# Weights split by casting and accumulating transfers, and Q, K and x moved by matmuls in the first groups of a recurrence-and-experts kernel

## The chip, the cores and the metric

The kernel runs on one core of a Trainium2 chip. The metric is the device time of one execution in microseconds, over several runs; a profiled execution gives the traces. TensorE (PE in the profile) multiplies matrices and writes PSUM; its weight loads have a row of their own (PEld). DVE and ACT do the elementwise work, POOL (GpSimd) fills and selects, and transfers are issued by SP's queue and POOL's.

## The reference

A linear recurrence per head with a complex decay, then a mixture of four dense experts:

```python
mag = np.sqrt(a_re * a_re + a_im * a_im)
scale = np.minimum(mag, 0.999) / (mag + 1e-06)       # a_re, a_im times scale
for t in range(S):
    S_re, S_im = ar * S_re - ai * S_im + kv, ar * S_im + ai * S_re   # kv = outer(k[t], v[t])
    y[:, :, t] = np.einsum('bhd,bhde->bhe', q[:, :, t], S_re)
x = y as [B*S, H*D] = [3072, 384]
p = domain_probs / (domain_probs.sum(-1) + 1e-09)
for e in range(4):
    out += p[:, e:e+1] * (np.maximum(x @ w1[e], 0) @ w2[e])          # w1[e]: 384 x 1024, w2[e]: 1024 x 384
```

There are 4 batches, 8 heads of 48, 768 steps. All data are float32.

## The kernel before

**Tiles.** The 3072 rows are cut into 12 groups of 256 (three per batch), a group into two chunks of 128. In the first part of the kernel every group goes through the recurrence ("attention" in the code) and then through experts 0 and 1; in the second part (lines 559 to 631) blocks of 512 rows go through experts 2 and 3 and the output is written. The second part isn't touched, except for a name.

**Weights.** The 32 weight tiles `w[i]` are 128 x 768: 384 columns of w1, then 384 rows' worth of w2. TensorE multiplies in its 32-bit matmul type (fp32r in the profile), which is shorter than float32, so each tile is held as a high part `whi` and a remainder `wlo`, and every product is a sum of three. `split_w` (L112) makes the two: a transfer by SP brings the tile (`wst`), ACT casts it (L115), and in the first part TensorE forms source minus high part in PSUM, by the identity and its negative (L125, L128), whence ACT copies it (L129). All 16 tiles of experts 0 and 1 are split before the first MoE matmul.

**The recurrence.** For each group DVE and ACT normalize the decay (`norm`, L276), form running products of it (`prefix`, L304) and from them the scaled queries Q and keys K (`finish`, L326), with the channels (head times 48) on partitions in three blocks of 128. The attention wants heads side by side instead, 48 rows at partitions 0 (real) and 64 (imaginary). That move goes through DRAM: `q_d`, `k_d` are written (L378) and read back into `Qst`, `Kst` (L383). In `chunk`, `increment` turns K (L411), copies it to `KT` and multiplies it with v (L416); `scores` multiplies `Kst` with `Qst` (L430) and DVE applies a mask (L433); `values` adds scores times v (L446) and state times Q (L442) in PSUM and copies y out (L454). y takes another trip through DRAM (`y_d`, L486, and `load_x`, L135) to come back as x with channels on partitions; `split_x` (L138) makes its high part `xha` (ACT) and remainder `xla` (DVE).

**The experts.** `moe1` goes over eight steps of two tiles: 18 matmuls of w1 (`w1_step`, L152), ReLU on ACT (L161), remainder on DVE (L162), 12 matmuls of w2 (`w2_step`, L171). `done` scales the sum and POOL stores it (L497).

**Order.** Each engine runs its instructions in the order that a scheduler gave them when the kernel was built; the program's order is its priority. `behind` fixes single orders. `attention` is a generator: while the block of group g - 1 runs, `between` lets one piece of group g's attention be issued ahead of steps `first`, `first + 1` and `first + 2`, with `first = max(2, 5 - g)` (L539). Group 0 has no block to hide behind. The probabilities `pr` are loaded by POOL at the start (L88) and reduced on DVE (L527). Tiles with the tag `tmp` share four buffers, `K` and `qk` have one, `A` two.

Of the kernel before, what the change touches and what calls it, by code (L numbers as in the profile page):

```python
# [29 lines left out]
NST = 4  # L30
# [25 lines left out]
NPRE = 10  # L56
NMID = 12
# [3 lines left out]
def fast_path(ctx, tc, qkP, aP, vP, probsP, w, out, flag):  # L61
# [8 lines left out]
    ident = const.tile([P, P], F32, name="ident")  # L70
    make_identity(nc, ident)
    nident = const.tile([P, P], F32R, name="nident")
    nc.scalar.activation(nident, ident, AF.Copy, scale=-1.0)
# [14 lines left out]
    nc.gpsimd.dma_start(pr, probsP.rearrange("(n p) e -> p n e", p=P))  # L88
# [5 lines left out]
    wts = {}  # L94

# [16 lines left out]
    def split_w(i, src, ps=None, prev=None, prev_pe=None):  # L112
        hi = wpool.tile([P, 2 * HD], F32R, tag="whi", name=f"whi{i}")
        lo = wpool.tile([P, 2 * HD], F32R, tag="wlo", name=f"wlo{i}")
        ins = nc.scalar.activation(hi, src, AF.Copy)  # L115
        if prev is not None:
            behind(ins, prev)
        if ps is None:
            nc.vector.tensor_tensor(lo, src, hi, op=ALU.subtract)
        else:  # L120
            pool, tag = ps
            for u in range(2):
                us = slice(u * HD, (u + 1) * HD)
                lp = pool.tile([P, HD], F32, tag=tag, name=f"lp{i}_{u}")
                ins = nc.tensor.matmul(lp, ident, src[:, us], start=True, stop=False)  # L125
                if prev_pe is not None:
                    behind(ins, prev_pe)
                last_pe = nc.tensor.matmul(lp, nident, hi[:, us], start=False, stop=True)  # L128
                nc.scalar.activation(lo[:, us], lp, AF.Copy)  # L129
        wts[i] = (hi, lo)  # L130
        return last_pe if ps is not None else None

    def load_x(g):
        x = moe.tile([P, NJ, G], F32, tag="x", name=f"xa{g}", bufs=1)
        nc.sync.dma_start(x, y_d[g].rearrange("(j p) t -> p j t", p=P))  # L135
        return x

    def split_x(g, x):  # L138
        xh = moe.tile([P, NJ, G], F32R, tag="xh", name=f"xha{g}")
        xl = moe.tile([P, NJ, G], F32R, tag="xl", name=f"xla{g}")  # L140
        tc.keep_in_program_order(nc.scalar.activation(xh, x, AF.Copy))  # L141
        tc.keep_in_program_order(nc.vector.tensor_tensor(xl, x, xh, op=ALU.subtract))
# [59 lines left out]
    with ExitStack() as c1:  # L202
# [4 lines left out]
        mask = big.tile([P, C], F32, name="mask")  # L207
# [6 lines left out]
        for i in range(SEG):  # L214
            nc.gpsimd.dma_start(maskp[i * CS:(i + 1) * CS], mask_d[:, i, :])
# [9 lines left out]
        nc.gpsimd.memset(Qst[32:IM], 0.0)  # L225
        nc.gpsimd.memset(Kst[32:IM], 0.0)
        nc.gpsimd.memset(KT, 0.0)
        nc.gpsimd.memset(P2, 0.0)
        nc.gpsimd.memset(TA, 0.0)

# [22 lines left out]
        def tmp(name):  # L253
            return big.tile([P, 2, NJ * G], F32, tag="tmp", name=name, bufs=TMP)

        def cmul(x, br, bi, shape, nm):
# [6 lines left out]
            v1 = tmp(f"{nm}a")[:, :, :n].rearrange(pat, **kw)  # L263
            v2 = tmp(f"{nm}b")[:, :, :n].rearrange(pat, **kw)
# [11 lines left out]
        def norm(g, A, parts=((0, SEG),), prev=(None, None)):  # L276
            s = tmp(f"s{g}")
            u = tmp(f"u{g}")
            for n, (lo, hi) in enumerate(parts):
# [5 lines left out]
                nc.scalar.activation(L, Af[:, 1], AF.Square)  # L285
# [5 lines left out]
                if n > 0:  # L291
                    behind(ins[0], idn)
                nc.scalar.activation(L, m2, AF.Ln, bias=m2b)
                nc.scalar.activation(y0, L, AF.Exp, scale=-0.5)
# [9 lines left out]
        def prefix(g, A, cuts=(1, NS)):  # L304
            for i in range(1, SEG):
# [6 lines left out]
                nc.vector.tensor_tensor(x[:, 1], z[:, 1, 0], z[:, 0, 1], op=ALU.add)  # L312
            k = 1
            while k < NS:
                nb = MS // (2 * k)
                Al = A[:, :, SEG - 1, :].rearrange("p c (b s) -> p c b s", s=2 * k)
                br, bi = (Al[:, c, :, k - 1:k].broadcast_to([P, nb, k]) for c in range(2))
                cmul(Al[:, :, :, k:], br, bi, [nb, k], f"sk{g}_{k}")
                k *= 2
            As = A.rearrange("p c i (j s) -> p c i j s", j=NJ)  # L320
# [5 lines left out]
        def finish(g, A, qk, parts=((0, CG),)):  # L326
            Q = big.tile([P, 2, NR, C + 1], F32, tag="tmp", name=f"Q{g}", bufs=TMP)
            K = big.tile([P, 2, NR, C], F32, tag="K", name=f"K{g}", bufs=1)
            s = tmp(f"s2{g}")
            u = tmp(f"u2{g}")  # L330
# [19 lines left out]
            for lo, hi in parts:  # L350
# [11 lines left out]
                if hi == CG:  # L362
                    nc.scalar.activation(Q[:, :, :, C].rearrange("p c (j n) -> p c j n", n=CG)[:, :, :, lo:],
                                         A[:, :, SEG - 1, NS - 1::NS].unsqueeze(3).broadcast_to([P, 2, NJ, hi - lo]),
                                         AF.Copy)
                a2, i0, t, kn = (some(x, lo, hi) for x in (a2a, i0a, ta, qk[:, 1]))
# [6 lines left out]
                scr = []  # L373
                for x, nm, w in ((Q, "q", C + 1 if hi == CG else C), (K, "k", C)):
                    dt = dram.tile([2, HD, hi - lo, w], F32, name=f"{nm}_d{g}_{lo}")
                    for c in range(2):
                        xs = x[:, c].rearrange("p (j n) t -> p j n t", n=CG)[:, :, lo:hi, :w]
# [18 lines left out]
        def chunk(g, c, K, y):  # L396
# [8 lines left out]
            def increment():  # L405
                if last:
                    return
# [416 lines left out]
```

## Time and profile before

| | us |
|---|---|
| median of 3 runs (lowest, highest) | 1032.83 (1031.87, 1033.28) |
| profiled execution, its own time | 1035.97 |
| its span, first to last instruction | 1034.2 |
| TensorE busy in it | 988.0 (96%) |
| DVE, ACT busy | 596.5, 358.9 |
| first MoE matmul starts | 74.27 |

A page has the busy time by engine, the span in 40 slices with digits for tenths, the transfers, the chain of work that ended last, and groups of instructions. `x` counts instructions; a time in brackets behind an arrow is idle time in front of an instruction and what ended it. In a group's line the first number behind the bar is busy time in us, the second the mean of one in ns. A float32 matmul shows as two records. Stretches are given in us from the start of the span.

### The profile page before, as it was taken

What the parts mean: (1) busy time and instruction counts of PE and PEld (TensorE: products, weight loads), DVE (VectorE), ACT (ScalarE), POOL (GpSimd) and SP (SyncE); (2) the same over time, 40 slices, a digit from 0 to 9 for tenths busy, and PEclk for the clock granted to TensorE, in tenths of its full rate; (3) what the DMA queues carried; (4) which work ended last, traced back from release to release, by engine and by line L of the source; (5) the groups of instructions that cost most, each with busy time, mean ns of one, the idle gap of its engine ahead of it and who ended that gap; (6) DMA issues with size and microseconds to landing.
All of it is one profiled execution on the core that took longest, in us unless ns stands there. A gap on an engine that the chain in (4) does not pass through costs nothing.

```text
span 1034.2 us, 15984 instructions
## 1 busy us (share of the span) xinstructions
PE 988.0 (96%) x6522; PEld 920.8 (89%) x6522; DVE 596.5 (58%) x1201; ACT 358.9 (35%) x647; POOL 27.8 (3%) x51
## 2 busy tenths in 40 slices
PE   4599889999999999999999999999999999999997
PEld 2379889898999999999999999999999999999996
DVE  6788877798988998888982264232232232321221
ACT  6845335352634635355342254121111111111110
POOL 4100000000000000000000000000000000000000
PEclk9989999999999999999999999999999999999999
DMA  7837372745658455483653493012030010100000
GB/s 257 217 113 155 107 197 80 191 115 141 165 139 199 120 149 152 120 203 126 145 123 78 129 360 123 1 41 82 1 110 13 22 71 1 61 1 1 31 1 34
DMA packets 79378, 113.12 MB, mean 109 GB/s; under 512 B 5440, under 2 KB 64496, under 8 KB 79296
## 3 DMA queue, kind: packets, MB, share of 16 engines
q1 hardware_dynamic: 76768, 101.61, 35.5%
q0 software_dynamic: 2528, 10.41, 2.8%
q8 instruction: 53, 0.87, 0.4%
q14 instruction: 29, 0.24, 0.1%
HBM read 74.11 MB, written 37.88 MB: 108 GB/s over the span
## 4 chain that ended last, share of the span: by engine, by line
PE 88%; DMA 6%; DVE 3%; ACT 1%; issue 1%; SPq 0%; DVEq 0%; POOL 0%; ACTq 0%; POOLq 0%
PE pob L598 19%; PE phb L585 19%; PE ph L152 18%; PE po L171 17%; PE sc L430 5%; PE dp L416 2%; PE yp L446 2%; PE yp L442 2%; DMA Kst<-k_d 2%; DMA k_d<-K 1%; PE ktp L411 1%; PE lp L125 1%; DMA pr<-probsP 1%; DMA q_d<-Q 1%; DMA xa<-y_d 1%
## 5 line engine op out<-in xcount | busy, mean ns | idle before, releaser
L591 DVE SCALAR_TENSOR_TENSOR hlb<-phb,hhb 128x512 fp32r<-128x512 f32 x96 | 66.3, 691 | 247.2 <-ACT hhb L590 247.2
L590 ACT ACTIVATE hhb<-phb 128x512 fp32r<-128x512 f32 x96 | 57.4, 598 | 314.2 <-PE phb L585 299.9
L171 PE MATMUL po<-whi,hh 128*128 128x384 f32 x384 | 129.2, 339 | 1.1 <-ACT hh L161 1.1
L598 PE MATMUL pob<-wlo,hhb 128*128 128x384 f32 x384 | 129.3, 337 | 0.0
L171 PE MATMUL po<-wlo,hh 128*128 128x384 f32 x384 | 129.1, 336 | 0.0
L598 PE MATMUL pob<-whi,hhb 128*128 128x384 f32 x384 | 128.9, 336 | 0.0
L171 PE MATMUL po<-whi,hl 128*128 128x384 f32 x384 | 123.1, 338 | 0.5 <-DVE hl L162 0.5
L598 PE MATMUL pob<-whi,hlb 128*128 128x384 f32 x384 | 117.8, 336 | 0.0
L152 PE MATMUL ph<-xha,whi 128*128 128x256 f32 x576 | 105.6, 288 | 4.1 <-ACT xha L141 4.1
L161 ACT ACTIVATE hh<-ph 128x512 fp32r<-128x512 f32 x96 | 57.2, 596 | 149.7 <-PE ph L152 146.1
L152 PE MATMUL ph<-xla,whi 128*128 128x256 f32 x576 | 103.5, 286 | 0.0
L152 PE MATMUL ph<-xha,wlo 128*128 128x256 f32 x576 | 101.4, 284 | 0.0
L162 DVE SCALAR_TENSOR_TENSOR hl<-ph,hh 128x512 fp32r<-128x512 f32 x96 | 66.0, 688 | 51.0 <-ACT hh L161 50.3
L152 PEld LDWEIGHTS ph<-xha,whi 128*128 128x128 f32 x576 | 87.2, 191 | 6.2 <-ACT xha L141 4.9
L585 PE MATMUL phb<-xhb,whi 128*128 128x512 f32 x288 | 91.8, 392 | 0.0
L152 PEld LDWEIGHTS ph<-xla,whi 128*128 128x128 f32 x576 | 83.6, 192 | 0.7 <-issue 0.6
L152 PEld LDWEIGHTS ph<-xha,wlo 128*128 128x128 f32 x576 | 83.2, 191 | 0.2 <-issue 0.2
L585 PE MATMUL phb<-xlb,whi 128*128 128x512 f32 x288 | 83.4, 392 | 0.0
L585 PE MATMUL phb<-xhb,wlo 128*128 128x512 f32 x288 | 82.1, 393 | 0.0
L598 PEld LDWEIGHTS pob<-wlo,hhb 128*128 128x128 f32 x384 | 72.1, 188 | 3.5
L598 PEld LDWEIGHTS pob<-whi,hhb 128*128 128x128 f32 x384 | 72.1, 188 | 3.4
L171 PEld LDWEIGHTS po<-whi,hh 128*128 128x128 f32 x384 | 72.6, 189 | 1.6 <-ACT hh L161 1.4
(142 smaller groups left out, 1568.9 us busy)
## 6 DMA issues: line engine op xcount, KB each, us to landing
wst<-w SPq DMA_DIRECT2D x32, 384.0 KB, 4.8
qk<-qkP SPq DMA_DIRECT2D x24, 384.0 KB, 7.0
acc_d<-acc POOLq DMA_DIRECT2D x24, 384.0 KB, 4.5
prev<-acc_d SPq DMA_DIRECT2D x24, 384.0 KB, 4.8
q_d<-Q SPq DMA_DIRECT2D x22, 387.0 KB, 3.8
Qst<-q_d SPq DMA_DIRECT2D x22, 387.0 KB, 5.6
A<-aP SPq DMA_DIRECT2D x22, 384.0 KB, 8.7
k_d<-K SPq DMA_DIRECT2D x22, 384.0 KB, 3.0
```

Source lines behind the costliest of these rows:

```text
L152: ins = nc.tensor.matmul(ph[:, u, :], wt[:, j * P:(j + 1) * P], xt[:, j, :], start=(n == 0), stop=(n == 3 * NJ - 1))
L161: nc.scalar.activation(hh, ph, AF.Relu)
L162: nc.vector.scalar_tensor_tensor(hl, ph, 0.0, hh, op0=ALU.max, op1=ALU.subtract)
L171: nc.tensor.matmul(po[t], ht[:, u, t * P:(t + 1) * P], wt[:, HD:], start=(i % FE == 0 and n == 0), stop=(i % FE == FE - 1 and n == 2))
L416: ins = nc.tensor.matmul(d_ps[:, h, :], KT[:, h, :], vc[:, h * D:(h + 1) * D], start=True, stop=True)
L430: nc.tensor.matmul(s_ps[:, h, :], Kc[:, hf * 4 + h, :], Qc[:, hf * 4 + h, :], start=True, stop=True)
L442: ins = nc.tensor.matmul(yo, state[g, c][:, h, :], Qc[:, h, :], start=True, stop=False)
L446: ins = nc.tensor.matmul(yo, vc[:, h * D:(h + 1) * D], sc[h // 4][:, h % 4, :], start=first, stop=True)
L585: nc.tensor.matmul(ph, wt[:, j * P:(j + 1) * P], xt[:, j, :], start=(n == 0), stop=(n == 3 * NJ - 1))
L590: nc.scalar.activation(hh, ph, AF.Relu)
L591: nc.vector.scalar_tensor_tensor(hl, ph, 0.0, hh, op0=ALU.max, op1=ALU.subtract)
L598: nc.tensor.matmul(po[t], ht[:, t * P:(t + 1) * P], wt[:, HD:], start=(i % FE == 0 and n == 0), stop=(i % FE == FE - 1 and n == 2))
```

## The change

**Weights of experts 0 and 1.** POOL issues 16 transfers that cast from float32 to the matmul type (`cast`) and so write `whi` directly. ACT writes its negative into `wlo`, and a second transfer by POOL adds the tile onto it. SP's loads, the identity matmuls and the copies from PSUM go. A small copy on POOL (`tick`) waits for the last part of the first decay tile ahead of the casts. The first ten negated copies are placed behind the first normalization, the other six behind xh of group 0. At the end the check that chooses between this path and a general one (a loop over the 768 steps) also asks that the largest remainder of tile 0 is above zero on every partition.

```diff
-    def split_w(i, src, ps=None, prev=None, prev_pe=None):
...
+    def cast(i):
+        whi[i] = wpool.tile([P, 2 * HD], F32R, tag="whi", name=f"whi{i}")
+        nc.gpsimd.dma_start(whi[i], w[i])
...
+    def split_w(i, prev=None):
+        lo = wpool.tile([P, 2 * HD], F32R, tag="wlo", name=f"wlo{i}")
+        ins = nc.scalar.activation(lo, whi[i].bitcast(F32), AF.Copy, scale=-1.0)
+        if prev is not None:
+            behind(ins, prev)
+        nc.gpsimd.dma_start(lo, w[i], accum_op=ALU.add)
+        wts[i] = (whi[i], lo)
```

**Q and K of groups 0 and 1 (`NSEL = 2`).** Q of chunk 0 of group 0, and K of chunk 1 of both groups, are moved by `pick`: matmuls whose stationary operand is 48 columns of a wide identity. K of chunk 0 is turned for the increment as before, and turned back head by head from `KT` into `Kst` (`turned_back`). The other parts of Q keep the trip through DRAM, all of it by SP. `blank` writes zeros into the rows between the two halves, since one copy now takes all 112 rows.

```diff
+        def blank(ps):
+            n, w = ps.shape[1:]
+            nc.tensor.matmul(ps[32:IM], zero, ident[0:1, 0:1].unsqueeze(2).broadcast_to([1, n, w]),
+                             start=True, stop=True)
+
+        def pick(g, nm, X, dst, s, w):
+            n = 4 if w == C else 3
+            for h0 in range(0, H, n):
+                hs = range(h0, min(h0 + n, H))
+                ps = ps_a.tile([M, len(hs), w], F32, tag="pa", name=f"{nm}p{g}_{s}_{h0}")
+                blank(ps)
+                for h in hs:
+                    js = [j for j in range(NJ) if -D < h * D - j * P < P]
+                    for j in js:
+                        o = 32 + h * D - j * P
+                        for c in range(2):
+                            nc.tensor.matmul(ps[c * IM:c * IM + D, h - h0, :], wide[:, o:o + D],
+                                             X[:, c, j * CG + s, :w], start=(j == js[0]), stop=(j == js[-1]))
+                nc.scalar.activation(dst[:, h0:h0 + len(hs), s, :w], ps, AF.Copy)
...
+            def turned_back():
+                for h0 in range(0, H, 4):
+                    ps = ps_a.tile([M, 4, C], F32, tag="pa", name=f"kp{g}_{c}_{h0}")
+                    for h in range(4):
+                        nc.tensor.transpose(ps[:, h, :], KT[:, h0 + h, :], ident)
+                    nc.scalar.activation(Kst[:, h0:h0 + 4, c, :], ps, AF.Copy)
```

**x of groups 0, 1 and 2 (`XSEL = 3`).** `turn_x` makes x in PSUM from y by matmuls with slices of a band of ones, six per chunk, and `split_x` reads it there. `y_d` is still written, for the second part; `values` blanks the rows between the halves of its PSUM tile for these groups (one more matmul per chunk).

```diff
+        def turn_x(g, c, y):
+            xp = ps_a.tile([P, NJ, C], F32, tag="pa", name=f"xp{g}_{c}")
+            for j in range(NJ):
+                ps = [p for p in range(HP) if -HOFF < 2 * D * p - P * j < P]
+                for p in ps:
+                    o = HOFF - (2 * D * p - P * j)
+                    state["xp"] = nc.tensor.matmul(xp[:, j, :], band[:, o:o + P], y[:, p, c * C:(c + 1) * C],
+                                                   start=(p == ps[0]), stop=(p == ps[-1]))
+            return slice(c * C, (c + 1) * C), xp
```

**Order.** For groups 0 and 1, prefix and finish run chunk by chunk (`front`), with the attention's pieces between them, and the last piece (turning K of chunk 1, its increment, the rotation of the state) comes behind the split of x. In `norm` of group 0 the squares of the second half are placed behind the first half's Exp. The steps at which pieces come are a table.

```diff
+FIRST = {1: 5, 2: 4, 3: 3, 4: 2}
...
+        def near_attention(g, QK):
+            Q, K = QK
+            y = small.tile([M, HP, G], F32, tag="y", name=f"y{g}")
+            (turn0, back0, inc0, sc0, val0), (turn1, back1, inc1, sc1, val1) = (chunk(g, c, K, y) for c in range(CG))
+            if g == 0:
+                pick(g, "q", Q, Qst, 0, C)
+                yield
+                landed = trip(f"q_d{g}", Q, Qst, 1)()
+            else:
+                landed = trip(f"q_d{g}", Q, Qst)()
+            yield landed
+            turn0()
+            back0()
+            sc0()
+            yield
+            pick(g, "k", K, Kst, 1, C)
+            inc0()
+            val0()
+            sc1()
+            xs = [turn_x(g, 0, y)]
+            val1()
+            xs.append(turn_x(g, 1, y))
+            yield xs
+            store_y(g, y)
+            t_factors()
+            turn1()
+            inc1()
+            rotate(g)
...
+        behind(nc.vector.reduce_sum(prs, pr, axis=mybir.AxisListType.X), ld)
```

`ld` is the last K product of group 0. Besides, the eight loads of the permuted mask move from POOL's queue to SP's, small products in `cmul` share one temporary tile, one wide identity takes the place of two, and POOL's fills change with the tiles (no fill of `Kst`, half of the one of `Qst`, a new band).

More of the change, by code (lines that the diff above doesn't have):

```diff
@@ L29 @@
 E1 = 2
-NST = 4
+NST = 6
 TMP = 4
@@ L403, in chunk, with turned @@
             sc = []
-            def increment():
-                if last:
+            def turned():
+                if last and g >= NSEL:
                     return
```

255 lines of the change are left out of this document (151 added, 104 removed).

## The prediction

> **What bounds the kernel now.** I read the page first, then busy time and granted clock by stretches, then the chain that ended last, then the waits of DVE and TensorE.
>
> ```profile
> span 1034.2 us, 15984 instructions
> ...
> PE   4599889999999999999999999999999999999997
> ```
>
> TensorE is the bound, but not everywhere: its row is full from the third slice on, apart from two 8s, and half empty in the first two. The stretches say it in microseconds (TensorE first, then its weight loads, DVE, ACT, POOL, granted clock, DMA share, GB/s).
>
> ```profile
> 10.00:20.00 10.00, 6.19 (x12) 3.02 (x11) 9.86 (x27) 7.97 (x16) 3.87 (x8) 1.00 0.96 367
> 52.00:74.20 22.20, 20.82 (x134) 16.25 (x132) 17.75 (x50) 10.38 (x23) 0.00 (x0) 0.87 0.42 127
> 74.20:120.00 45.80, 45.66 (x372) 44.09 (x373) 41.75 (x88) 19.59 (x37) 0.58 (x1) 1.00 0.52 126
> 120.00:166.00 46.00, 38.87 (x305) 36.37 (x303) 35.25 (x79) 18.57 (x35) 1.10 (x2) 0.96 0.51 138
> 166.00:212.00 46.00, 43.92 (x335) 42.37 (x334) 36.69 (x79) 20.71 (x39) 1.08 (x2) 0.96 0.55 147
> 212.00:258.00 46.00, 44.48 (x357) 42.92 (x355) 38.80 (x84) 20.00 (x38) 0.54 (x1) 0.96 0.54 141
> ```
>
> From 74.2 to 258 TensorE is idle for 0.14 + 7.13 + 2.08 + 1.52 = 10.9 us, and in three stretches it has 0.96 of its clock, 3 x 46 x 0.04 = 5.5 us more: 16.4 us lost. So the end is the start of the first MoE matmul, plus TensorE's work behind it, plus these losses. The chain shows how that start comes about (start, length).
>
> ```profile
> 1.39 8.25 DMA pr<-probsP
> ...
> 11.64 0.61 ACT s L293
> ...
> 12.85 0.42 ACT u L294
> ...
> 37.80 0.33 DVE u L367
> 38.13 7.53 DMA k_d<-K
> ...
> 46.67 4.67 DMA Kst<-k_d
> ...
> 72.86 0.50 ACT wlo L129
> ...
> 73.37 0.85 ACT xha L141
> ...
> 74.27 1.82 PE ph L152 x13
> ```
>
> Three things stretch it: DVE waits for the router probabilities, K takes a round trip through DRAM, and the weight splits stand in front of xh. DVE's waits before 75, and the end of its K:
>
> ```profile
> DVE scs L433 <- PE sc L430: 7.2, 2, 6.8
> DVE prs L527 <- DMA pr<-probsP: 4.8, 1, 4.8
> ```
>
> ```profile
> 39.48 1.03 DVE L371 TENSOR_TENSOR K<-A,u 128x384 f32<-128x384 f32 x2
> ```
>
> TensorE's waits after 74.2, by who ended them:
>
> ```profile
> PE sc L430 <- DMA Kst<-k_d: 4.9, 2, 2.8
> PE ph L152 <- ACT xha L141: 4.1, 2, 2.6
> PE sc L430 <- issue: 2.3, 3, 1.5
> ```
>
> **The head, step by step.** The reduction over the probabilities moves behind the last K product, so DVE no longer sits idle for 4.8 us until the transfer lands at 9.6. Late next are ACT's Ln and Exp of the first half (0.61 and 0.42), which the change puts ahead of the squares of the second half: normalizing begins near 6 in place of 9.7. I move K's end by 4 us, from 40.5 to 36.5. The first chunk's K is ready one tail earlier (2.7 us, from 37.8 to 40.5 in the trace), at 33.8.
>
> From there no transfer of K and no reload of x is on the path; TensorE is. Its prices:
>
> ```profile
> L430 PE MATMUL sc<-Qst,Kst 112*128 112x128 f32 x384 | 55.0, 299 | 15.9 <-DMA Kst<-k_d 13.5 <-issue 2.3
> L446 PE MATMUL yp<-scs,v 128*48 128x128 f32 x384 | 36.1, 275 | 0.0
> L416 PE MATMUL dp<-v,KT 128*112 128x48 f32 x320 | 34.4, 258 | 1.3 <-issue 1.3
> ...
> L125 PE MATMUL lp<-wst,ident 128*128 128x384 f32 x64 | 29.5, 550 | 13.5 <-DMA wst<-w 9.6 <-ACT wlo L129 3.7
> ...
> L411 PE MATMUL ktp<-ident,K 128*128 128x128 f32 x120 | 18.1, 276 | 0.0
> ```
>
> ```profile
> 109.05 0.39 PE L446 MATMUL yp<-scs,v 128*48 128x128 f32 x4
> 109.27 0.39 PE L442 MATMUL yp<-Qst,G 112*48 112x128 f32 x4
> ```
>
> A float32 matmul is two records. A full one on 128 columns costs at most 2 x 55.0/384 = 0.29 us; I take 0.25, since that union holds each group's drain. A 48-wide one costs between 0.11 (four records, two matmuls, start 0.22 apart) and 0.19 (2 x 36.1/384); the selection matmuls alternate between the same two halves of the output, so 0.11. A transpose is at most 18.1/120 = 0.15, taken as 0.12; an increment matmul at most 2 x 34.4/320 = 0.21, taken as 0.2. A matmul that blanks the rows between the halves streams 512 columns from one row: four times 0.25 is 1.0; by the 384 columns of L125, 2 x 29.5/64 x 512/384 = 1.2 at most.
>
> A pick is 20 selection matmuls (eight heads, two of which straddle a block of 128, times two components) and two blanks: 2.2 + 2.0 = 4.2 us (6.2 at the other price). The band takes six full matmuls per chunk, 1.5 (1.7). Turning KT back is eight transposes, 1.0 (1.2). Behind 33.8 stand: turn 0.7, back 1.0, scores 2.0, pick of K 4.2, increment 1.6, values 0.9 and blank 1.0, scores 2.0, band 1.5, values with the state 1.8 and blank 1.0, band 1.5: 19.2 us. Handovers at the end (mask, y out of PSUM, xh) add about 2, and TensorE, without the splits that kept it at work, starts colder: 2 more. MoE starts at 33.8 + 19.2 + 4 = 57; between 52 (nothing for handover and cold, some work done early) and 62 (upper prices). The head gives 74.3 - 57 = 17.3 us.
>
> Q of the second chunk keeps its trip:
>
> ```profile
> q_d<-Q SPq DMA_DIRECT2D x2, 193.5 KB, 6.2
> Qst<-q_d POOLq DMA_DIRECT2D x2, 193.5 KB, 6.4
> ```
>
> Issued near 31 it lands near 44, before the second scores near 47; if it takes longer, they wait. The mask loads move to SP's queue, where they wait for the mask's store; behind them stand only the loads of v and this trip, needed 20 us later: nothing.
>
> **What ACT sheds and gets.** The splits' 64 + 32 TensorE records lay before 74.3, so no TensorE work behind it goes away.
>
> ```profile
> L129 ACT ACTIVATE wlo<-lp 128x384 fp32r<-128x384 f32 x32 | 14.7, 486 | 11.2 <-PE lp L128 11.1
> L115 ACT ACTIVATE whi<-wst 128x768 fp32r<-128x768 f32 x16 | 12.6, 831 | 1.1 <-DMA wst<-w 1.1
> L454 ACT ACTIVATE y<-yp 48x512 f32<-48x512 f32 x4 | 2.4, 592 | 4.4 <-PE yp L446 4.4
> ```
>
> These 27.3 us become 16 negated copies at 0.79, 12.6 us; pick and turn give back some six copies out of PSUM at 0.6. Ten negated copies may run any time after the first normalization, and each waits at the head of ACT's queue for its casting transfer, with Ln, Exp and the copies of Q and K behind it. Six are tied behind xh of group 0 and stand ahead of the first ReLU, 4.7 us, covered by two weight steps and the increment that moves there. On POOL each accumulation waits for its negated copy; behind it stand only the stores of acc, which nothing reads before the second half of the kernel.
>
> **Work that TensorE gains behind its new start.** Group 1: pick 4.2, back 1.0, two blanks 2.0, two bands 3.0, in all 10.2. Group 2: blanks and bands 5.0. The last turn and increment of group 0 (6 x 0.12 + 8 x 0.2 = 2.3) slide behind the start. Sum 17.5; with upper prices 21.8.
>
> **What becomes of the 16.4 us.** The 4.1 in front of xh go where x comes from the band. The waits for Kst stay for groups from 2 up, which keep the DRAM trip. DVE gets to its next group about 9 us earlier (4 from above, some 5 of the 7.2 for the scores), TensorE 17 earlier with 10 more to do in group 1: about even. The pieces of groups 1 to 3 also come one step of the block later, which gives a late Kst some 4 us. I keep 6 us, clock included.
>
> **Sum.** -17.3 + 17.5 - 16.4 + 6 = -10.2 on the profiled span of 1034.2, so 1024.0. The median of the runs shown, 1032.83, lies below that span; the same difference gives 1022.6. I say 1022. A head at 52 without losses gives 1011; one at 62 with 6 us more of them, 1034.
>
> **The transfers.** No casting or accumulating one is in this trace. Nearest rows:
>
> ```profile
> q0 software_dynamic: 2528, 10.41, 2.8%
> ```
>
> ```profile
> acc_d<-acc POOLq DMA_DIRECT2D x24, 384.0 KB, 4.5
> ```
>
> ```profile
> L215 POOL DMA_DIRECT2D maskp<-mask_d x8 | 3.9, 492 | 4.6 <-DMA mask_d<-mask 4.6
> ```
>
> By the first, 10.41 MB took 16 engines for 0.028 x 1034 = 29 us, 1.1 us for one tile of 384 KB, and the stretch from 10 to 20 ran at 367 GB/s, which says the same. The 4.5 us to landing is the far end, should such transfers not overlap. I take 1.1 for a cast and 2.2 for an accumulation, which reads its destination too: 16 x 3.3 = 53 us, from about 10 to 63, while the last tile is wanted near 110. The Trainium skill, "Collectives: The Full Stack", section "The bandwidth ceiling: the fold count and why AG ≠ RS ≠ AR", says that an add in the transfer costs its second read and not the arithmetic, 1.93 to 1 where it was measured; the sum would be the same, and no run here shows it yet.
>
> **Rivals.** *Slower: the tiles come late.* A block is a stretch of 46 us less some 12 of attention at the prices above, 34; with group 1's attention of about 24 in between, its last step comes near 57 + 58 - 5 = 110. If a tile takes r us for cast and add and the last is ready at 10 + 16 r, TensorE waits from r = 6.3 on, and at 7 the gain is gone; at r = 9 (4.5 twice, no overlap) it is 1022 + 44 = 1066. Against it: the 1.1. For it: ACT's queue, where one late cast holds all behind it. Chance 0.13. POOL's issues took 0.49 us each in the row above, beside a DVE busy for 9.86 of 10 us. The Trainium skill, "SBUF — State Buffer", section "SBUF: two separate sides", warns that descriptors made by GpSimd starve while DVE holds the port they share, 620 ns becoming 3100; that row does not show it, and 32 such issues, 99 us, would just stay within the 110.
>
> *No change: DVE's chain, not the head, times the first groups.* DVE is full for 41.75 of 45.8 us from 74.2 to 120; TensorE then starts earlier only to wait longer, and all 16.4 us of losses stay: -17.3 + 17.5, 1033. For it: Kst ends most of today's waits. Against: DVE's chain itself moves by 9. Chance 0.14.
>
> *The change does not do what it says.* If a cast to the matmul's type leaves the value whole, the remainder is zero, the new test at the end finds no positive one, and the general loop of 768 steps runs as well: thousands of microseconds. Chance 0.02.
>
> *More: a head near 52 and no losses,* 1008 to 1014. Chance 0.09.
>
> **How the numbers follow.** Forecast 0.62 (1014 to 1029). A measurement of this kernel tells about 0.2%, 2 us. Faster: 0.62 + 0.09 + 0.03 of the second rival; same 0.08 of it; slower 0.03 of it, 0.13 and 0.02. The range leaves out most of the first rival, the third, and the end of the fourth: 1010 to 1036.
>
> **What would show it.** Right: the first ph matmul near 57, K's last product near 36.5, no wait over 2 us for xh of groups 1 and 2, some 17 us more of small matmuls, wlo landing ahead of use. Wrong: ACT's negated copies wait long for casts, ph or po waits for wlo, or TensorE's waits from 60 to 250 pass 16 us.

## The result, and the profile after

The changed kernel is slower. On one chip it took 1049.34 us (median of 4 runs, 1047.10 to 1051.01) against 1032.35 us for the kernel before (median of 4): a ratio of 1.0162, 95% interval 1.0142 to 1.0183. Its profiled execution took 1049.73 us, with a span of 1048.0.

The page of the changed kernel: the span, TensorE's row and the granted clock by slice.

```profile
span 1048.0 us, 16221 instructions
...
PE   1689999998999999999999999999999999999997
...
PEclk9989998999989999999999999999999999999998
```

TensorE is full from the fourth slice on, one slice later than before, although MoE starts earlier. The transfers of its head; first POOL's queue as a whole (packets, megabytes, share of the 16 engines), then by name (count, size, median us to landing):

```profile
q0 software_dynamic: 6624, 22.14, 7.5%
...
whi<-w POOLq DMA_DIRECT2D x16, 384.0 KB, 8.2
wlo<-w POOLq DMA_DIRECT2D x16, 384.0 KB, 10.1
...
q_d<-Q SPq DMA_DIRECT2D x2, 193.5 KB, 13.1
Qst<-q_d SPq DMA_DIRECT2D x2, 193.5 KB, 4.4
```

The store of Q's second chunk, 6.2 us before, takes 13.1. The stretches (same columns as in the prediction) show what it shares the DMA engines with, and what TensorE does meanwhile:

```profile
30.00:40.00 10.00, 8.35 (x58) 5.93 (x55) 7.47 (x19) 6.49 (x13) 3.39 (x4) 1.00 1.10 210
40.00:52.00 12.00, 7.42 (x74) 6.19 (x73) 4.54 (x11) 4.54 (x7) 0.00 (x0) 0.86 0.95 195
52.00:74.20 22.20, 18.25 (x135) 16.70 (x136) 14.34 (x30) 9.34 (x19) 5.30 (x6) 0.82 0.59 145
```

From 30 to 40 the DMA engines are full (1.10), and from 40 to 52 TensorE (busy for 7.42 of 12) and DVE (4.54 of 12) both stand idle for much of the time. The chain of waits names the transfer:

```profile
34.09 0.94 DVE Q L398 x2
35.25 15.06 DMA q_d<-Q
50.32 3.45 DMA Qst<-q_d
53.91 3.75 PE sc L484 x16
...
65.17 0.49 ACT xha L144
65.66 4.40 ACT wlo L122 x6
```

K and the reload of y are gone from the chain, as the change intends, and Q's trip has taken their place. The 16 records of scores behind it take 3.75 us, where the first chunk's 16, at 35.98 and at full clock, took 2.05: TensorE runs at half clock after its wait, with 0.50 granted from 52.7 to 59.6. DVE stands behind the same trip, because in its order the masking of those scores comes ahead of the rest of group 1's normalization; the 4.16 us ahead of it are a wait for ACT's Exp:

```profile
47.92 0.96 DVE L311 TENSOR_TENSOR u<-s,u 128x768 f32<-128x768 f32 x1 [4.16 <-ACT u L309]
55.99 0.69 DVE L487 TENSOR_TENSOR scs<-sc,maskp 128x512 f32<-128x512 f32 x1 [7.11 <-PE sc L484]
...
99.77 1.02 DVE L412 TENSOR_TENSOR K<-A,u 128x384 f32<-128x384 f32 x2
```

Group 1's K is done at 100.8; before, it was done at 93.4. TensorE's waits of the changed kernel:

```profile
PE sc L484 <- DMA Qst<-q_d: 6.5, 1, 6.5
...
PE sc L484 <- issue: 5.5, 3, 3.0
...
PE ph L157 <- ACT xha L144: 0.6, 1, 0.6
```

**Where the time went.** Stretches from one group's first ph matmul (its first MoE matmul) to the next's tell lead, work and losses apart. Before:

```profile
74.30:124.20 49.90, 47.26 (x380) 45.36 (x380) 43.61 (x91) 20.42 (x38) 0.58 (x1) 1.00 0.51 128
124.20:173.50 49.30, 44.74 (x346) 42.55 (x347) 37.60 (x81) 20.60 (x38) 1.10 (x2) 0.97 0.51 137
173.50:223.50 50.00, 47.92 (x366) 46.38 (x366) 42.64 (x90) 26.14 (x49) 1.08 (x2) 0.97 0.51 136
223.50:273.50 50.00, 48.48 (x381) 46.92 (x380) 42.95 (x90) 23.06 (x42) 1.08 (x2) 0.97 0.59 157
```

After:

```profile
65.70:128.40 62.70, 60.38 (x462) 54.83 (x461) 49.28 (x132) 27.46 (x55) 6.44 (x8) 0.95 0.47 108
128.40:185.10 56.70, 54.32 (x403) 49.78 (x403) 45.96 (x100) 21.64 (x41) 1.09 (x2) 0.94 0.45 121
185.10:229.00 43.90, 43.90 (x352) 42.52 (x353) 37.86 (x80) 20.92 (x38) 0.54 (x1) 1.00 0.58 150
229.00:281.30 52.30, 48.75 (x383) 46.64 (x382) 44.74 (x96) 25.12 (x47) 1.08 (x2) 0.97 0.56 144
281.30:330.00 48.70, 47.28 (x359) 45.86 (x358) 38.74 (x81) 21.76 (x40) 1.08 (x2) 0.93 0.56 146
```

MoE starts 74.3 - 65.7 = 8.6 us earlier. Over six blocks before (to 364.1; the fifth and sixth lost 0.75 us) the losses are 11.5 us of idle time plus 4.5 of clock (49.3, 50 and 50 at 0.97), 16.0. Over six blocks after (to 377.6; the sixth lost 1.15) they are 10.8 of idle time plus 11.5 of clock, 22.3. The six take 311.9 us in place of 289.8: 22.1 more, 6.3 of it losses and so some 16 work. With -8.6 that makes 13.5 of the 13.8 us between the spans; the later blocks and the second part of the kernel together have nearly their old length (670.4 us from there on, 670.1 before).

### The profile page after: what moved, and what is told of

The parts are those of the page before. It is cut to its first block, busy times and chain, and to the rows that moved or that the text cites. A ratio compares the mean times of both kernels' runs of the same rounds, so it can differ in the third digit from the quotient of the medians.

```text
span 1048.0 us, 16221 instructions
## 1 busy us (share of the span) xinstructions
PE 997.0 (95%) x6658; PEld 929.4 (89%) x6658; DVE 599.5 (57%) x1219; ACT 348.7 (33%) x623; POOL 43.4 (4%) x75
## 4 chain that ended last, share of the span: by engine, by line
PE 86%; DMA 6%; DVE 4%; ACT 2%; issue 1%; SPq 0%; DVEq 0%; ACTq 0%
PE pob L733 19%; PE phb L720 19%; PE ph L157 17%; PE po L176 17%; PE sc L484 5%; PE dp L472 2%; DMA q_d<-Q 2%; PE yp L502 2%; PE yp L498 2%; DMA Kst<-k_d 1%; PE ktp L456 1%; DMA Qst<-q_d 1%; PE xp L533 1%; PE yp L345 1%; DMA k_d<-K 1%
## 5 line engine op out<-in xcount | busy, mean ns | idle before, releaser
L167 DVE SCALAR_TENSOR_TENSOR hl<-ph,hh 128x512 fp32r<-128x512 f32 x96 | 66.0, 687 | 59.7 <-ACT hh L166 59.4
```

The lines of the kernel that those rows point to most:

```text
L167: nc.vector.scalar_tensor_tensor(hl, ph, 0.0, hh, op0=ALU.max, op1=ALU.subtract)
```

## The experiments

Three theories were tested. **A**: the casting and accumulating transfers slow Q's trip, and that loses the head. **B**: the chain of DVE, with its waits, times the next groups, whatever the head does. **C**, formed later: a short wait just ahead of a stretch of small matmuls halves the clock, and those matmuls do not bring it back. The runs were on other chips, where the kernel before took 1037 to 1039 us, so ratios to it are compared; the changed kernel itself ran on the first chip alone. Times within a kernel are those of its profiled run.

**All of group 0's Q picked.**

```diff
-                landed = trip(f"q_d{g}", Q, Qst, 1)()
+                pick(g, "q", Q, Qst, 1, C + 1)
+                landed = state["v"]            # the load of v
```

> Changed kernel, but Q of group 0's second chunk is moved by selection matmuls too (three blanks, 20 selections, some 5 us of TensorE) in place of the trip through DRAM. Theory A (the head loses to Q's trip beside the casting transfers, and what TensorE is given behind it costs in full): the 6.5 us wait before the second scores goes, the half clock behind it too, DVE's 7.1 us wait with them; the first ph comes at 60 to 63 in place of 65.7 and the whole gain of 3 to 5 us stays: 1044 to 1046. Rival B (DVE's chain times the first groups): DVE gains 7, so group 1 starts 7 or more earlier: 1042 or less. Rival C (the head is bound elsewhere, mask or ACT): first ph stays at 65 to 66, 1049.

Measured: 0.9996 (0.9970 to 1.0022), 1.6% better than the changed kernel. First ph at 58.3, group 1's K at 89.4, the wait gone. The head gains 16 us on the kernel before and the end nothing. A's first half holds; so does B's number for the end.

**The new moves for group 0 alone**, first with Q's trip, then with Q picked.

```diff
-NSEL = 2
-XSEL = 3
+NSEL = 1
+XSEL = 1
```

> Changed kernel with the new moves for group 0 alone: groups 1 and 2 take the trips through DRAM as before (10.2 and 5.0 us of TensorE work less). Theory A (TensorE's added work is what eats the head): group 1's interval falls from 62.7 to some 53, group 2's from 56.7 to 51, and the end comes 10 to 15 us earlier, 1034 to 1039. Rival B (DVE's chain sets group 1's start; its K is done at 100.8, and before the change 30.8 us passed from there to the group's first ph): group 1 starts at 128 to 132 as now, the saved work becomes waiting, 1044 to 1050.

Measured: 1.0091 (1.0056 to 1.0127), group 1's first ph at 127.2: between the two, as A's 1034 to 1039 us are 1.002 to 1.006 of 1032.35, and B's 1044 to 1050 are 1.011 to 1.017.

> The run in which all of group 0's Q is picked, with the new moves for group 0 alone (groups 1 and 2 take the trips as before; 15 us of TensorE work less). DVE has group 1's K at 89.4 in that run, against 93.4 in the kernel before. Theory B (DVE's chain times the next groups, head or no head): group 1's first ph comes some 30.8 us behind that K, 118 to 122 as with the added work, the work turns into waits, and the end is at 1030 to 1034 by the span of before, ratio 0.996 to 1. Rival A (the added work is what ate the lead): 15 us less work are 10 to 15 us, ratio 0.985 to 0.99.

Measured: 1.0018 (0.9995 to 1.0041), group 1's first ph at 116.8, 1.2 us earlier than B's bound, group 4's at 273.5 as before. Its waits on TensorE:

```profile
PE sc L484 <- DMA Kst<-k_d: 7.0, 4, 3.5
...
PE sc L484 <- issue: 5.7, 3, 2.9
PE ph L157 <- ACT xha L144: 5.2, 2, 4.6
```

Fifteen us less of TensorE work are worth 7 us beside a late DVE and nothing beside an earlier one: they turned into waits for K and x. A's second half (added work costs in full) falls.

**Two pieces of the change alone, on the kernel before.** The order of the sum and of the norm:

```diff
-        nc.vector.reduce_sum(prs, pr, axis=mybir.AxisListType.X)
+        behind(nc.vector.reduce_sum(prs, pr, axis=mybir.AxisListType.X), ld)
...
-                    behind(ins[0], idn)
+                    behind(ins[0], exp)
+                    behind(sq, exp)
```

> Kernel before with one piece of the change: the sum over the router probabilities goes behind the last product of K, and Ln and Exp of the first half of group 0 ahead of the squares of the second half. Theory A: DVE's wait of 4.8 us goes and everything behind it comes 3 to 4 us earlier, first ph near 70.5, 1029. Rival C (the head is bound by the weight splits on ACT and TensorE): first ph stays at 73 to 74, 1032 to 1033.

Measured: 0.9992 (0.9971 to 1.0014), first ph at 73.3. DVE starts 4 us earlier, but K of group 0 ends at 39.8 against 40.5, and the second chunk's waits go on as they were. The number is that text's rival C, and the trace bears it out: from 27.5 to 30.6 DVE waits 3.1 us for two squares on ACT, which stand behind the weight splits in ACT's queue. The lead is spent there.

The weights:

```diff
-            split_w(i, wst[i] if i < NST else stage1(i, PRE), (ps_o, "po"), nrm)
+            split_a(i, nrm)      # negated copy, accumulating transfer; cast(i) ahead of the first norm
```

> Kernel before with one piece of the change: the 16 tiles of phase 1 are cast by one transfer and completed by an accumulating one (no weight splits on TensorE, one copy each on ACT). Theory A (the casting and accumulating transfers slow the trips beside them, as Q's from 6.2 to 13.1 us): the trip of K in the head takes 5 us and more longer, Kst lands 52 to 58 in place of 51.3, and what the splits give back goes there: first ph at 72 to 78, 1031 to 1037. Rival D (no contention to speak of): the trip keeps its 12 us, ACT and TensorE are free when y is there, first ph at 70 or less, 1027 to 1029.

Measured: 1.0000 (0.9985 to 1.0015). The trip of K is slowed far beyond the forecast: Kst lands 9.6 us later, and first ph comes at 84.7, 10.4 us later than before. The wait, and the stores of Q beside it (3.2 us to landing before):

```profile
PE sc L443 <- DMA Kst<-k_d: 23.6, 5, 18.2
```

```profile
q_d<-Q SPq DMA_DIRECT2D x2, 192.0 KB, 13.1
```

Yet the end does not move. The first block of this run has 0.3 us of idle time, where the first two of the kernel before had 2.6 and 4.6:

```profile
84.70:131.80 47.10, 46.84 (x369) 45.59 (x370) 42.66 (x90) 23.35 (x42) 0.58 (x1) 0.95 0.54 138
```

A head 10 us later was absorbed whole: the losses of the kernel before are time in which TensorE waits for DVE's chain.

**DVE lightened**, in the kernel before and in the one with Q picked.

```diff
-            for i in range(1, SEG):
+            for i in range(1, 1 if 1 <= g <= 4 else SEG):
```

> Kernel before, leaving out the running products over the eight segments in groups 1 to 4 (21 DVE operations a group, 7 x (0.56 + 0.26 + 0.25) = 7.5 us of DVE each); nothing on TensorE changes, and the output is another. Theory B (DVE's chain times groups 1 to 4 of the kernel before; the 16.4 us that TensorE loses there are its lateness): the waits for Kst and xh and the half clocks go, 8 to 13 us: ratio 0.987 to 0.992. Rival A (the losses are latencies of trips and handovers, which a shorter DVE chain does not touch): ratio 0.997 to 1.

Measured: 1.0164 (1.0131 to 1.0197), against B. Group 4's first ph came 5.8 us earlier, less than B said; then, with the products back, everything was lost:

```profile
DVE Q L360 <- DMA qk<-qkP: 24.2, 5, 10.0
```

DVE had run ahead in its order, and stood for up to 10 us for the load of qk, with the blocks' hl behind it in its order. The end of this run says nothing on B.

> The run in which all of group 0's Q is picked, with the same running products left out for groups 1 to 4. It has 9.9 us of idle time and 8.7 us of lost clock from its first ph to group 5's. Theory B (DVE's chain makes these too): they fall to some 6, and the head's lead stays: ratio to before 0.985 to 0.99, no better than the light kernel before by more than its lead less the added work (16 - 17.5 = -1.5). Rival A (TensorE's added small matmuls lose the clock and the time by themselves): 0.996 to 1.

Measured: 0.9925 (0.9895 to 0.9954). Group 4's first ph at 259.3, 13.4 us earlier than with the full DVE work; one half-clock stretch is left of four. From first ph to group 5's, idle time and lost clock are 5.6 us, where the text said some 6. That is B, with the ratio a little short of its range.

**DVE's work given to POOL**, likewise in both.

```diff
-                nc.vector.tensor_tensor(Af, Af, bc2(y0), op=ALU.mult)
+                (nc.gpsimd if g > 1 else nc.vector).tensor_tensor(Af, Af, bc2(y0), op=ALU.mult)
...
-                nc.gpsimd.dma_start(acc_d[g][e], acc)
+                nc.scalar.dma_start(acc_d[g][e], acc)
```

(and the first two products of `rotate` from group 1 on.)

> Kernel before, with three DVE operations a group given to POOL from group 1 on: the product of A with the norm (1.76 us, from group 2) and the first two of the turning of the state (2 x 0.55); the stores of acc move to ACT's queue. DVE's work from group 0's K to group 4's falls from 154 us by some 8. Theory B (DVE's chain times groups 1 to 4, and group 4's first ph at 273 is its mark): that mark comes 4 to 8 us earlier, ratio 0.992 to 0.996. Rival (it is the ring of K's trip and scores, not DVE's work): no change, 0.998 to 1.002. A slow POOL operation that DVE then waits for would hide either: then A waits on POOL show it.

Measured: 1.0073 (1.0049 to 1.0097), a miss. POOL takes 3.5 us for DVE's 1.76, and DVE then waits for it:

```profile
L309 DVE TENSOR_TENSOR pf<-A 128x384 f32<-128x384 f32 x84 | 46.6, 554 | 14.6 <-POOL A L301 12.9
```

> The run in which all of group 0's Q is picked, with the same operations given to POOL. Theory B: group 4's first ph, at 272.7 there, comes 4 to 8 us earlier; as TensorE's own bound lies at 58.3 + 185 + 17.5 = 261, that can be had: ratio 0.992 to 0.997. Rival (added TensorE work and half clocks are the bound of this one): 0.999 to 1.003.

Measured: 0.9961 (0.9943 to 0.9979), group 4's first ph at 269.5 in place of 272.7, a gain a little under B's. The two together fit a B in which DVE's chain counts with its waits, and not by its busy time alone.

**The casts held back**, with Q's trip kept.

```diff
-        for i in range(NF1):
+        for i in range(6):
             cast(i)
...
         norm(1, A[1], prev=(la, ld))
+        hold = nc.gpsimd.tensor_copy(tick, state["K"][0:1, 1, NR - 1, 0:1])
+        for i in range(6, NF1):
+            behind(cast(i), hold)
...
-EARLY = 10
+EARLY = 6
```

> Changed kernel, with ten of the 16 casting transfers held back until the last product of group 0's K (a copy on POOL reads that tile first), the accumulations behind them, so that Q's trip has the DMA engines to itself but for six accumulations. Theory A (the trip was slowed by the casting and accumulating transfers beside it): from issue to landing its store takes 6 to 8 us in place of 13.1, the wait before the second scores falls to under 2 us, first ph at 59 to 61, and, by theory B (what DVE's chain gains, the end gains), the end is 6 to 11 us earlier than the changed kernel's: ratio to before 1.004 to 1.01. Rival (the trip is slow by itself, in its shape or on SP's queue): the wait stays at 5 us or more, ratio 1.014 to 1.018. The weights should come in time; if ph waits for wlo, that shows in TensorE's waits.

Measured: 0.9957 (0.9934 to 0.9979): better than forecast there, and faster than the kernel before. First ph at 58.5. The trip and its surroundings:

```profile
q_d<-Q SPq DMA_DIRECT2D x2, 193.5 KB, 3.4
```

```profile
30.00:40.00 10.00, 6.38 (x50) 5.48 (x47) 8.53 (x19) 6.34 (x12) 0.39 (x1) 0.91 0.24 63
```

With the DMA engines at 0.24 in place of 1.10, the same store, issued at 34.4 against 34.8, lands in 3.4 us in place of 13.1. Group 1's K is done at 85.7. No ph or po waited for the later weights. The Trainium skill, "Trainium Kernel Development and Optimization", section "Key Constraints", says that transfers issued from SP, ACT and POOL run on the same 16 engines and interleave; these two rows agree.

The edit moves one thing more: the mask's store stood behind all 16 casts on POOL's queue and was issued at 22.6; now it goes at 11.8, and DVE's wait of 2.5 us for the mask goes too. That is not what shortens the store of Q: in the changed kernel the mask had landed by 38.0 and the store took until 50.3, and in the run with the weights alone, where the mask's loads are on POOL's queue, Q's stores took 13.1 us too.

**The late negated copies spread** behind the ReLUs of group 0, on top of the held casts, and the same without the band for group 2.

```diff
-        for i in range(EARLY, NF1):
-            split_w(i, wts["x"])
+        late = iter(range(EARLY, NF1))
...
                 def between(k, g=g, pieces=pieces, first=first, last=last):
+                    if g == 1:
+                        for _, i in zip(range(3), late):
+                            split_w(i, wts["h"] if k else wts["x"])     # "h": the last ReLU
```

> The run with casts held back, and the ten later negated copies of wlo spread behind the ReLUs of group 0's first steps in place of standing in one bunch ahead of them (in the held run TensorE waits 2.8 us for KT behind them at 63.1, with half clock from 65.4 to 72.4, 3.5 us more). If that bunch was on the path: both go, up to 6 us at group 1's first ph (119.5 there); as DVE's chain (its K of group 1 at 85.7) hardly moves, at most 2 to 4 us reach the end, ratio to before 0.992 to 0.994. Rival (DVE's chain and its waits alone time the end): no change from the held run, 0.995 to 0.997.

> The same, with x of group 2 reloaded from DRAM again (two blanks and two bands less, 5 us of TensorE). If TensorE's work is now the bound: 3 to 5 us less than the run with three groups, ratio lower by 0.003 to 0.005. If the chain of DVE and its waits is: the reload's wait for xh at group 2 (2 to 4 us) takes its place, ratio the same within 0.002 or up to 0.002 higher.

Measured: 1.0105 (1.0077 to 1.0134) and 1.0121 (1.0082 to 1.0159). Both theories missed: the first is 15 us slower than the held run by the ratios, and 21 us by the profiled spans (the held run's profile is the fastest of its runs). Group 1's K is 4.4 us later (90.1), and this happens in front of its attention:

```profile
95.67 3.42 PE L484 MATMUL sc<-Qst,Kst 112*128 112x128 f32 x16 [2.05 <-ACT Kst L465]
```

```profile
93.00:96.00 3.00, 0.95 (x7) 0.63 (x6) 2.33 (x2) 1.29 (x4) 0.00 (x0) 1.00 1.00 304
96.00:100.00 4.00, 4.00 (x18) 2.96 (x16) 2.34 (x6) 1.60 (x4) 0.00 (x0) 0.51 0.40 157
...
112.00:116.00 4.00, 4.00 (x34) 3.29 (x33) 1.46 (x6) 0.00 (x0) 0.00 (x0) 0.50 0.01 4
116.00:120.00 4.00, 4.00 (x28) 4.00 (x29) 2.54 (x8) 0.72 (x2) 0.00 (x0) 0.93 0.18 49
```

A wait of 2.05 us, and the clock is at half for 20.5 us, through scores, picks, increment and values, with TensorE busy all the time: 10 us lost, and DVE waits behind it in turn. From this came theory C, and three runs that move group 1's pieces.

The traces also show the clock fall with no wait ahead, which theory C does not have. In the changed kernel it is at half from 114.2 to 117.6, and TensorE had no gap over 0.3 us in the 8 us before. These matmuls stand there:

```profile
110.18 1.30 PE L359 MATMUL kp<-K,wide 128*48 128x128 f32 x20
111.41 1.77 PE L472 MATMUL dp<-v,KT 128*112 128x48 f32 x16
113.11 1.04 PE L345 MATMUL yp<-wide,zero 1*32 1x512 f32 x2
...
114.50 0.65 PE L502 MATMUL yp<-scs,v 128*48 128x128 f32 x4
```

The last row takes 0.65 us where the same four records take 0.39 at full clock. Nine half-clock stretches of these runs began in this way, with TensorE busy for all of the 3.4 us before, and each time all 16 records of an increment and some of a blank lay in these 3.4 us. Not every increment does this: the last run below has no such stretch.

**Pieces of group 1 one step later or earlier.**

```diff
-FIRST = {1: 5, 2: 4, 3: 3, 4: 2}
+FIRST = {1: 6, 2: 4, 3: 3, 4: 2}        # 4 in the second of the three
```

> The run with the spread copies (K of group 1 at 90.1, TensorE idle for 2.1 us before group 1's scores at 95.7 and then at half clock for 20.6 us), with group 1's pieces one step of the block later (4.2 us of MoE matmuls more ahead of its scores). Theory C (a wait of 2 us just ahead of a stretch of small matmuls lets the clock fall, and the small matmuls do not bring it back; that, 10 us, and DVE's waits behind it made the loss against the held run): the wait and the 20.6 us at half clock go, group 1's first ph at 119 to 121, and the ratio to before comes back to 0.995 to 1.001. Theory B alone (DVE's K of group 1, 4.4 us later than in the held run, sets the end): 1.003 or more.

Measured: 1.0029 (0.9996 to 1.0063), first ph of group 1 at 117.7. The wait and the 20.5 us are gone, and about half of the loss with them (8 us of 15 by the ratios, 11 of 21 by the spans); the rest stays, with a wait of 2.0 us at 143.7 ahead of group 2's scores and 10.2 us at half clock behind that. Between the two theories.

> The held run, where no wait stands before group 1's scores (K at 85.7, scores at 93.3), with group 1's pieces one step earlier. Theory C: TensorE now waits 1 to 3 us for K ahead of them, the clock is at half for 10 to 20 us through group 1's attention, and the end is 8 to 20 us later, ratio 1.004 to 1.015. Theory B alone: the wait costs what it lasts and DVE's chain absorbs it: 0.995 to 0.999.

Measured: 1.0118 (1.0077 to 1.0159), as C says and B does not. The made wait is there:

```profile
PE sc L484 <- DMA Qst<-q_d: 2.5, 1, 2.5
```

The profiled run, 1037.59 us, is the shortest of its runs: only 3.4 us at half clock follow the wait, and the mean granted clock is 0.988. Three others had 0.980, 0.975 and 0.974: 0.008, 0.013 and 0.014 of 1049 us are 8, 14 and 15 us, and they took 9, 12 and 14 us longer (1046.93, 1049.43 and 1051.47). What varies from run to run is the clock. The others have no trace, so where they lost it, behind the made wait or elsewhere, isn't shown.

> The held run with group 1's pieces one step later. No wait stood there, so nothing is to be won: theory C says the same as the held run within 3 us, 0.993 to 0.999; theory B says 1 to 4 us later (scores later, DVE waits for them): 0.997 to 1.001.

Measured: 0.9900 (0.9863 to 0.9936), the lowest ratio of all, and better than both theories said: something was to be won where no wait stood, and what it was isn't shown. First ph only at 63.9, with 17.1 us at half clock in the head, where the held run, with the same matmuls in the same order, has 3.4; but none behind 77 us, apart from the one that every run has as it ends.

**The later step alone, and all three together.**

> Changed kernel with group 1's pieces one step later and nothing else. Theory A (Q's trip beside the casting transfers is what failed): its 6.5 us wait, DVE's waits behind it and K of group 1 near 100 stay, so it stays 10 us and more above the run with casts held and pieces later: ratio to before 1.008 to 1.018. Theory C alone (the place of the pieces decides, since it decides the clock): it comes to 0.99 to 1.002 as that run did.

Measured: 1.0099 (1.0077 to 1.0122): within A. Q lands as late as in the changed kernel (its store takes 13.1 us; TensorE, at half clock from 37.6, waits only 1.5 us of it), group 1's K is done at 96.5, and a wait of 2.1 us ahead of group 1's scores is again followed by 20.5 us at half clock. The profiled run, 1057.89 us, is the slowest of its five; the others took 1046.30 to 1051.02.

> Casts held, group 1's pieces one step later, and all of group 0's Q picked as well. Nothing waits for a trip in the head then. Its head has 5 us more of TensorE work and no half clock behind a wait; first ph near 58 to 60, and group 1's K near 86: ratio 0.986 to 0.992, the same as the run with casts held and pieces later or a little less. Rival (TensorE's added work in the head delays the scores and DVE by its 5 us): 0.993 to 0.997.

Measured: 0.9918 (0.9896 to 0.9939), first ph at 60.3, group 1's K at 87.4: as good as the best within the intervals. A trip through clear DMA engines does as well as 5 us of matmuls.

The marks of all runs: first ph of group 0, end of group 1's K, first ph of group 4, in us of the profiled run, and the ratio.

| run | group 0 | K of group 1 | group 4 | ratio |
|---|---|---|---|---|
| before | 74.3 | 93.4 | 273.5 | 1 |
| changed | 65.7 | 100.8 | 281.3 | 1.0162 |
| order of sum and norm alone | 73.3 | 92.5 | 272.7 | 0.9992 |
| weights alone | 84.7 | 99.3 | 273.6 | 1.0000 |
| Q picked | 58.3 | 89.4 | 272.7 | 0.9996 |
| group 0 alone | 62.8 | 98.4 | 280.4 | 1.0091 |
| group 0 alone, Q picked | 59.4 | 89.3 | 273.5 | 1.0018 |
| before, DVE lightened | 75.7 | 82.9 | 267.7 | 1.0164 |
| Q picked, DVE lightened | 58.6 | 84.0 | 259.3 | 0.9925 |
| before, work to POOL | 74.4 | 93.6 | 275.4 | 1.0073 |
| Q picked, work to POOL | 58.7 | 88.2 | 269.5 | 0.9961 |
| casts held | 58.5 | 85.7 | 267.8 | 0.9957 |
| casts held, copies spread | 58.4 | 90.1 | 284.6 | 1.0105 |
| the same, no band for group 2 | 58.6 | 90.1 | 278.4 | 1.0121 |
| casts held, copies spread, pieces later | 58.5 | 89.7 | 276.7 | 1.0029 |
| casts held, pieces earlier | 58.5 | 84.9 | 274.0 | 1.0118 |
| casts held, pieces later | 63.9 | 91.0 | 269.2 | 0.9900 |
| pieces later alone | 62.8 | 96.5 | 289.6 | 1.0099 |
| all three | 60.3 | 87.4 | 266.3 | 0.9918 |

Five kernels whose heads end anywhere from 58 to 85 us, with 0 to 17 us of added work, reach group 4 within 1 us of each other (before, the two single pieces, and the two rows with Q picked and no other edit than the groups'). DVE's K of group 1 does not fix that mark by itself: 99.3 goes with 273.6, and 100.8 with 281.3. Its K of group 4 goes with it better: it ends at 228.8 to 233.3 in the five, and at 243.6 in the changed kernel.

## Why the prediction was wrong

The sum made against the span was 1024.0 and the span was 1048.0: 24 us, of which 8.7 are the head's term and 16 the losses'.

**The head.** The step that failed is "Issued near 31 it lands near 44, before the second scores near 47; if it takes longer, they wait." The store was issued at 34.8, Q landed at 53.8, and TensorE lost 6.5 us in the wait and 2.9 by half of the 5.7 us at half clock behind it: 9.4 us. About 1 us of the wait would have come in any case, since ACT's last copy into Kst ended at 48.4; with its old times the trip would have landed at 47.4. The rest of that term held. From the turn of K at 32.75 to first ph at 65.7 are 33.0 us; less those 9.4, 23.6 against the 23.2 forecast (19.2 of work and 4 of handovers). K's last product came at 41.9 and not at 36.5, after 2.5 us of waiting for the mask, whose move was priced at nothing: its store stood behind the 16 casts on POOL's queue. TensorE had other work until 47.4, so the head did not lose by it, but DVE came to group 1 later. What was missing is a sentence between two parts of the prediction: the transfers were priced at 53 us of full DMA engines from 10 to 63 (7.5% of 1048 less the 29 us before is 50, so the price was right), and Q's trip, in the middle of just that stretch, was given its old 6.2 + 6.4 us. The run with the casts held shows that this was the cause: the store, issued at the same time, took 3.4 us.

**The work behind the start.** Forecast 17.5, measured some 16. That it filled waits, or became waits when taken away, was not seen: it was added to the sum as if TensorE were the bound there.

**The losses.** The step "DVE gets to its next group about 9 us earlier", and from it "I keep 6 us, clock included", failed. DVE's K of group 1 came 7.4 us later: 1.4 because group 0's K did, and 6 because DVE waited longer between the two, 17.6 us in place of 11.9. Of the 7.2 us for the scores, 5 were to go, and 7.1 stayed, since the masking of the late ones stands ahead of the normalization; the wait for ACT's Exp grew from 2.4 to 4.2, and 2.4 for xha are new. Waits stayed at 11 us and half clocks grew from 4.5 to 11.5. Even where DVE was 4 us earlier (Q picked), the waits stayed, and the time was that of the second rival, 1.00, to which the prediction gave 0.14. Its mechanism, DVE's chain timing the first groups, is borne out by the lightened run (group 4 at 259.3 in place of 272.7), though the two runs that lightened the kernel before could not show it. One thing is to be added: the end of DVE's K moves with the head's last transfer, so a late trip costs twice.

**The clock.** The prediction lists half clocks as losses that go with the waits. They do not: small matmuls behind a short wait carried them on, and nine times small matmuls began one with no wait ahead.

**The rivals on the other side.** The weights came in time; nothing waited for `wlo`. The slower case was put on the new transfers' own lateness, and it came from what they do to an old one, so 1049 lay outside the range. With the trip clear of the casts and the pieces later, the ratio is 0.990, and 1022 was 0.990 of 1032.83. That the two agree is in part luck: in that run's profile the head gives 10.4 us and not 17.3, the losses over six blocks fall from 16.0 to 8.3 and not to 6, and the added work comes to 14 and not 17.5.

**Open.** How much of the spread between the runs is DVE's chain and how much the clock is not settled: each makes the other, and the runs with the spread copies lie between the two. Nor is it shown why the later step helps the held run, or which small matmuls let the clock fall. Whether casting or accumulating transfers hurt a trip more wasn't tried.

## What to carry to other kernels

When a change adds transfers, list every old transfer that runs in the same stretch and price it anew. A start that comes earlier is worth only what the next engine in the chain can follow; look for the kernel's fixed mark (here group 4) before counting a head's gain. Leave no wait, however short, just ahead of a stretch of small matmuls: put dense work there, until the data is in. Even without a wait, read the granted clock behind small matmuls before counting their time.

## What the runs showed of the hardware

- Casting and accumulating transfers of 384 KB, 16 of each in a row, landed 8.2 and 10.1 us after issue; POOL was busy for 0.55 and 1.07 us a piece beside a busy DVE.
- A store of two transfers of 193.5 KB took 13.1 us to landing beside them, 6.2 beside the old weight loads, and 3.4 with the DMA engines at 0.24.
- The granted clock fell to half and stayed there in steps of about 3.4 us. It fell behind waits of TensorE from 1.0 us on (240.6 to 241.6 with copies spread and pieces later), and nine times with no wait in the 3.4 us before, in small float32 matmuls. It stayed down for 20.5 us when small float32 matmuls followed a wait of 2.05 us, though TensorE was busy in all of it. The Trainium skill, "TensorE: Matmul & The Clock Gate", section "Part 1: The HAM clock gate (the "warmup" mystery)", says that an idle window of about 3.4 us halves the clock and one busy window of that length brings it back; here a wait of 2.05 us was enough for the first, and six busy windows were not enough for the second.
- The same product, 128 x 1536, took 1.76 us on DVE and 3.5 on POOL.
